# Dilated local attention as banded 121-key matmuls with an unshifted exp, in place of VectorE products over shifted keys

## Chip, core, metric

One NeuronCore of a Trainium2 chip (trn2). The metric is the device time of one execution in microseconds; the kernel before takes 307.15 us (median of 4 runs, 306.28 to 307.87).
A *state* is given with each run: fast or slow. A single core shows a slow state in a few executions here (342.45 against 337.4 to 338.3 us for the changed kernel). Only fast runs are compared.
A ratio below is, as far as it can be recomputed, the mean time of an experiment's fast runs over that of the kernel before in the same rounds on the same chip, without the profiled run, so it is not quite the ratio of the medians that are quoted.

## The reference, cut to what matters

2048 tokens of 448 features; 16 heads of 28. Every query sees 8 keys: itself and the tokens 2, 4, ... 14 before it.

```python
def _A_ref(x, wqkv, wo):                      # attention
    H = 16; Dh = D // H; W, dil = 8, 2
    q, k, v = split(x @ wqkv)
    idx = pos[:, None] - arange(W)[None, :] * dil
    logits = einsum("bhsd,bhswd->bhsw", q, k[idx]) * Dh ** -0.5   # masked where idx < 0
    o = einsum("bhsw,bhswd->bhsd", softmax(logits), v[idx])
    return merge(o) @ wo

def _B_ref(x, w1, w2, w3, w4):                # mixer and MLP
    h = gelu(layernorm(x) @ w1)
    hs = concat(four quarters of h, shifted by +1, -1, +2, -2 tokens) @ w2
    x1 = x + hs
    return x1 + gelu(layernorm(x1) @ w3) @ w4

h  = x + _A_ref(layernorm(x), A_wqkv, A_wo)
h2 = h + _B_ref(layernorm(h), B_w1, B_w2, B_w3, B_w4)
```

## The kernel before

Instructions are not written in the order in which they run. Each helper (`mm`, `act`, `dve`, `pool`, `dma`) puts an operation with an *estimated duration* on a list; a list scheduler then fixes one static order per engine, and semaphores are derived from it. Each engine's program holds its instructions in that order, whatever the real durations are.

Attention of a tile of 512 tokens:

```python
        def phase_A2(t):
            for c in range(4):           # q times 8 shifted copies of k: one 112x4096 product each
                dve("tensor_tensor", 4096, out=ring(slot)..., in0=q_b, in1=k_s, op=ALU.mult)
            for c in range(4):           # sum over the 28 features of a head, with an indicator matrix
                for a8 in range(8):
                    mm(L, zc[:, c, ...], ring(slot)[:, a8 * 512:(a8 + 1) * 512], first, last, 512)
            # row maximum, subtract, exp, sum, reciprocal of 128x64, scale ...
            dma(..., Pd[t * 128:(t + 1) * 128, :], pb[:, sl, :], 128 * 1024)   # probabilities to memory
            # ... and back, each row copied to the 28 partitions of its head (64 loads of 224 KB)

        def phase_A3(t):
            for c in range(4):           # probabilities times 8 shifted copies of v
                dve("tensor_tensor", 4096, out=r4, in0=r4, in1=v_s, op=ALU.mult)
            for c in range(4):           # sum over the 8 keys: identity matmuls
                for w in range(NW):
                    mm(ps[0:KC, b, :], ident[0:KC, 0:KC], r4[:, :, w, :], w == 0, w == NW - 1, 512)
                act(actT[:, a, c, :], ps[0:KC, b, :], ACT.Copy, 512)
            # ... output projection with wo; x is added by one more identity matmul
```

Layer norms use three Newton steps of tiny VectorE instructions for the inverse deviation, and ScalarE for the normalisation. Part B (`B1`: w1 and gelu, `B2`: w2, residual, statistics, `W3`: w3 and gelu, `B3`: w4 and output) begins on the first tiles while attention of the last is still under way.

## Time and profile before

| | before |
|---|---|
| time, median | 307.15 us |
| last attention result written | about 171 us |
| matmuls of part B dense | from 206 us |
| mean granted TensorE clock | 0.961 |

The page of the profiled execution: the busy time, the slices (40 equal slices of the span, each digit the busy share of a slice in tenths, PEclk the granted TensorE clock in tenths) and the chain that ended last.

```profile
span 306.6 us, 3389 instructions
...
PE 260.6 (85%) x1297; PEld 136.4 (44%) x1297; DVE 168.8 (55%) x346; ACT 154.7 (50%) x240; POOL 19.7 (6%) x44
...
PE   0499959959995799996777988949899999989996
...
DVE  3659889983799728985762789001801640200221
...
PEclk9999979979999599998999999986999999999999
...
PE 53%; DVE 27%; ACT 15%; issue 3%; DMA 1%
```

TensorE is busy nearly everywhere. VectorE is busy in the first half and idle in the second. Groups of instructions, shapes kept apart (busy us, mean ns of one, then idle time before them and its releasers):

```profile
L630 DVE TENSOR_TENSOR arena<-arena 112x4096 bf16<-112x4096 bf16 x32 | 72.0, 2287 | 17.6 <-PE ps L630 9.5 <-DMA arena<-attn_p_scratch 7.5 <-ACT arena L630 0.3
...
L630 DVE RECIPROCAL rz<-zs 128x64 f32<-128x64 f32 x4 | 2.2, 553 | 0.1
```

The second line is small here: a reciprocal of 64 columns takes 553 ns. Two windows (length; busy time of PE, PEld, DVE, ACT, POOL with the number of instructions; granted clock; DMA share; GB/s): attention from 25 to 171 us, and the last part.

```profile
25.00:171.00 146.00, 124.10 (x597) 66.76 (x596) 111.12 (x179) 78.46 (x125) 0.21 (x2) 0.94 0.55 127
...
206.00:304.00 98.00, 94.85 (x488) 46.92 (x486) 24.59 (x66) 41.59 (x65) 12.07 (x12) 0.97 0.06 18
```

Attention and the start of part B share the first window, and TensorE is 85% busy in it (124.10 of 146).

### The profile page before, as it was taken

What the parts mean: (1) busy time and instruction counts of PE and PEld (TensorE: products, weight loads), DVE (VectorE), ACT (ScalarE), POOL (GpSimd) and SP (SyncE); (2) the same over time, 40 slices, a digit from 0 to 9 for tenths busy, and PEclk for the clock granted to TensorE, in tenths of its full rate; (3) what the DMA queues carried; (4) which work ended last, traced back from release to release, by engine and by line L of the source; (5) the groups of instructions that cost most, each with busy time, mean ns of one, the idle gap of its engine ahead of it and who ended that gap; (6) DMA issues with size and microseconds to landing.
All of it is one profiled execution on the core that took longest, in us unless ns stands there. A gap on an engine that the chain in (4) does not pass through costs nothing.

```text
span 306.6 us, 3389 instructions
## 1 busy us (share of the span) xinstructions
PE 260.6 (85%) x1297; PEld 136.4 (44%) x1297; DVE 168.8 (55%) x346; ACT 154.7 (50%) x240; POOL 19.7 (6%) x44
## 2 busy tenths in 40 slices
PE   0499959959995799996777988949899999989996
PEld 0254435526542365452444554425445544544552
DVE  3659889983799728985762789001801640200221
ACT  1522346446730567524897568695663167066000
POOL 4000000000000000000000005002205002300000
PEclk9999979979999599998999999986999999999999
DMA  7900018837850299915885000000000100100111
GB/s 224 327 4 0 3 32 202 197 84 175 195 112 0 63 200 207 205 33 145 196 178 191 0 0 2 0 1 0 2 0 30 33 0 0 47 15 0 32 45 45
DMA packets 11824, 24.71 MB, mean 81 GB/s; under 512 B 1376, under 2 KB 9120, under 8 KB 10016
## 3 DMA queue, kind: packets, MB, share of 16 engines
q1 hardware_dynamic: 11808, 24.50, 32.6%
q8 instruction: 10, 0.16, 0.2%
q14 instruction: 6, 0.05, 0.1%
HBM read 22.13 MB, written 2.36 MB: 80 GB/s over the span
## 4 chain that ended last, share of the span: by engine, by line
PE 53%; DVE 27%; ACT 15%; issue 3%; DMA 1%
PE ps L630 53%; DVE arena L630 17%; ACT actT L630 7%; ACT lntm L630 4%; ACT arena L630 3%; DVE st L630 3%; DVE rs_t L630 1%; DVE rs_y L630 1%; DMA xin<-in_A_x_dram 1%; DVE mv L630 1%; DVE ls L630 1%; ACT ls L630 1%; DVE mx L630 1%; ACT L630 0%; DVE rs_x L630 0%
## 5 line engine op out<-in xcount | busy, mean ns | idle before, releaser
L630 PE MATMUL ps<-actT,arena 112*128 112x512 bf16 (+1 forms) x416 | 100.8, 404 | 17.2 <-ACT actT L630 16.6
L630 ACT ACTIVATE arena<-ps 112x512 bf16<-112x512 f32 (+1 forms) x114 | 68.0, 597 | 46.4 <-PE ps L630 46.3
L630 DVE TENSOR_TENSOR arena<-arena 112x4096 bf16<-112x4096 bf16 x32 | 72.0, 2287 | 17.6 <-PE ps L630 9.5
L630 PEld LDWEIGHTS ps<-actT,arena 112*128 112x128 bf16 (+1 forms) x416 | 48.7, 121 | 66.7 <-ACT actT L630 22.2
L630 ACT ACTIVATE actT<-ps 112x1024 bf16<-112x1024 bf16 (+1 forms) x40 | 32.6, 846 | 29.5 <-PE ps L630 29.5
L630 DVE TENSOR_TENSOR ost<-ps,arena 128x448 bf16<-128x448 f32 x16 | 10.0, 625 | 64.6 <-PE ps L630 64.6
L630 PE MATMUL ps<-arena 128*128 128x448 bf16 x224 | 42.9, 353 | 0.0
L630 ACT ACTIVATE lntm<-xin,nbias,rs_y 128x448 bf16<-128x448 bf16 x32 | 22.9, 750 | 17.6 <-DVE nbias L630 17.6
L630 PEld LDWEIGHTS ps<-arena 128*128 128x128 bf16 x224 | 21.9, 98 | 20.7
L630 PE MATMUL ps<-arena,ident 112*112 112x512 bf16 x128 | 28.8, 380 | 0.8 <-DVE arena L630 0.8
L630 PE MATMUL ps<-arena,zc 112*128 112x512 bf16 x128 | 28.3, 380 | 0.0
L630 DVE BATCH_NORM_STATS2 st<-xin 128x6 f32<-128x448 bf16 x32 | 19.3, 604 | 15.6 <-ACT xin L630 11.0
L630 PE MATMUL ps<-ident,lntm 128*112 128x128 bf16 x192 | 15.5, 229 | 13.9 <-ACT lntm L630 13.8
L630 POOL TENSOR_TENSOR arena<-arena,xin 128x448 f32<-128x448 f32 x16 | 16.1, 1035 | 110.8 <-ACT lntm L630 110.8
L630 PE MATMUL ps<-wo_s,actT 112*128 112x448 bf16 x64 | 17.2, 379 | 6.7 <-ACT actT L630 6.4
L630 PE MATMUL ps<-actT,w_s 112*112 112x512 bf16 x64 | 18.6, 441 | 4.6 <-ACT actT L630 4.6
L630 PEld LDWEIGHTS ps<-arena,ident 112*112 112x112 bf16 x128 | 16.5, 130 | 11.9 <-DVE arena L630 1.3
L630 PEld LDWEIGHTS ps<-ident,lntm 128*112 128x112 bf16 x192 | 14.0, 136 | 17.2 <-ACT lntm L630 15.0
L630 DVE TENSOR_TENSOR arena<-ps,arena 128x448 f32<-128x448 f32 x16 | 9.6, 599 | 21.7 <-PE ps L630 21.6
L630 PEld LDWEIGHTS ps<-arena,zc 112*128 112x128 bf16 x128 | 12.4, 98 | 15.0 <-issue 0.2
L630 ACT ACTIVATE ls<-ls 128x512 f32<-128x512 f32 x4 | 2.5, 630 | 28.4 <-DVE ls L630 28.4
L630 PEld LDWEIGHTS ps<-actT,w_s 112*112 112x112 bf16 x64 | 9.0, 150 | 12.2 <-ACT actT L630 6.6
(39 smaller groups left out, 134.4 us busy)
## 6 DMA issues: line engine op xcount, KB each, us to landing
arena<-attn_p_scratch SPq DMA_DIRECT2D x64, 224.0 KB
arena<-in_B_w_dram SPq DMA_DIRECT2D x2, 1568.0 KB, 11.5
xin<-in_A_x_dram SPq DMA_DIRECT2D x4, 448.0 KB, 8.2
out_dram<-ost SPq DMA_DIRECT2D x16, 112.0 KB, 1.7
arena<-in_A_wqkv_dram SPq DMA_DIRECT2D x1, 1176.0 KB, 7.4
w_s<-in_B_w_dram SPq DMA_DIRECT2D x2, 392.0 KB, 8.8
attn_p_scratch<-pb SPq DMA_DIRECT2D x4, 128.0 KB, 1.8
wo_s<-in_A_wo_dram SPq DMA_DIRECT2D x1, 392.0 KB, 10.3
```

The source lines that it names most:

```text
L630: inst = getattr(eng, op.meth)(**op.kw)
```

## The change

The intent: take attention off VectorE and out of memory. Tokens are split into even and odd ones, so that the 8 keys of a query are 8 neighbours of the same parity. A block of 114 queries then needs 121 keys. One *unit* is 3 blocks for 4 heads; 2 parities x 3 groups x 4 channels of heads make 24 units. Per unit TensorE computes full 121x114 scores, exp is taken without a row maximum, a 0/1 mask keeps the band, and two sets of matmuls give the outputs and, replicated over 32 partitions, the sums. If an intermediate leaves the floating-point range, a flag sends every engine into the old program, which is kept behind a branch. The core of the diff:

```diff
+    ring = {"st": [(0, 1, 2, 3), 0], "oz": [(4, 5), 0], "gen": [(6, 7), 0]}     # the 8 PSUM banks
+    def phase_att(par, g):
+        for c in range(4):
+            for blk in range(3):                       # scores: 12 matmuls, 28 rows each
+                for j in range(4):
+                    mm(ps[0:KB, j, blk * QB:(blk + 1) * QB], kT[32 * j:32 * j + 28, ...],
+                       qT[32 * j:32 * j + 28, ...], True, True, 40)
+            act(pt[0:KB, sl, :, :], ps[0:KB, 0:4, 0:GQ], ACT.Exp, 4 * GQ, scale=SCALE)
+            dve("tensor_tensor", 4 * GQ, 2.0, out=pt..., in0=pt..., in1=m_, op=ALU.mult)
+            bo, bz = bank("oz"), bank("oz")
+            # ... outputs into bo: 12 matmuls (121 rows, 32 columns of weights, 114 moving)
+            # ... sums into bz: 12 matmuls of the same shape, with ones as weights
+            dve("reciprocal", GQ, psum=True, out=rzb[:, u % 2, :], in_=ps[:, bz, 0:GQ])    # GQ = 342
+            dve("scalar_tensor_tensor", GQ, psum=True, out=oT..., in0=rzb[:, u % 2, :],
+                scalar=UP, in1=ps[:, bo, 0:GQ], op0=ALU.mult, op1=ALU.mult)
 ...
+    phase_att(0, 0)
+    phase_QK(1)
+    phase_V(1, 0)
+    phase_A1(2)
+    phase_att(1, 0)
+    phase_QK(2)
 ...                                    # all six attention phases, then
+    for t in range(NST):
+        phase_B1(t)
+    # flag from the exponent bits of the statistics
+    phase_B2(0)
+    phase_B2(1)
+    phase_W3(0)
 ...
+                        emit_fast(e, eng)
+                        eng.wait_ge(flag_op.sem, flag_op.val)
+                        with eng.register("redo_" + e) as reg:
+                            eng.reg_load(reg, flag[0:1, 0:1])
+                            with eng.If_ne(reg, 0):
+                                # ... the old program
```

Besides, the inverse deviation becomes a power on GpSimd, normalisation moves from ScalarE to VectorE, and the weights of part B are loaded at the start. The scheduler is told 523 ns for the reciprocal.

## The prediction

> **What bounds it now.** The busy table gives PE 260.6 us (85%), VectorE 168.8, ScalarE 154.7 of a 306.6 us span; the chain of waits is 53% matmuls, 27% VectorE, 15% ScalarE. The last attention result is written at about 171 us (timeline; part B starts overlapping it at 147). In it VectorE is nearly saturated (windows 20-60 and 80-100 us: 19 of 20 us busy), mainly the 32 products of 112x4096 (2287 ns each, 72.0 us in all). From 206 us on, matmuls are dense (94.9 of 98 us).
>
> **Removed.** The 32 large VectorE products (72 us), max/subtract/sum/scale (about 12 us), the 128+128 reducing and summing 512-column matmuls, 16 residual matmuls, the scratch round trip through memory (14 MB read back), the Newton chains (about 25 us of tiny VectorE instructions, now a power on GpSimd). A dense chain of 166 matmuls took 33.03 us, 199 ns each; so the 256 reduction matmuls are about 51 us of PE time. The normalisations leave ScalarE (45 us) for VectorE in a faster mode (estimate 0.27 us bf16, 0.35 us f32: 20 us).
>
> **Added: 24 units (2 parities x 3 groups x 4 channels).** Costs, estimated from trace durations:
> - PE: 36 small matmuls, each with its weights. Sixteen transpose pairs of like size took 1.05 us, 66 ns each; so 2.4 us without concurrency, perhaps 1.5 us with it: 36-57 us in all. The Trainium skill (TensorEngine Tiling, Key Properties) says changing tiling mode drains the engine; no run shows it yet.
> - ScalarE: exp of 121x1368; evictions of 512 and 1024 columns (597, 1016 ns) give 170 ns + 0.82 ns a column: 1.3 us, 31 us in all.
> - VectorE: mask 0.87 us (2287 ns scaled); product with the inverse 0.5 us; and the reciprocal. The trace has 128x64 at 553 ns where an instruction on four columns takes 162: over 6 ns a column. The Trainium skill (VectorE: DVE Perf Modes, the fixed hardware budget) says reciprocal is an iterative divide, repeat count 8; the trace agrees in kind. For 342 columns: about 2.3 us, not the 0.5 us that the new scheduler is told; 55 us in all. VectorE per unit: 3.7 us, 90 us in all.
>
> **Where it lies.** One pair of output/sum banks serves all units, so each waits for the reciprocal and product of the one before: mask, 24 matmuls, reciprocal, product form a loop of 4.5-5 us; VectorE fills its gaps with statistics and residual adds (about 27 us). Attention becomes VectorE-bound: about 25 us of start plus 24 x 4.8, ending near 140 us instead of 171. Then part B: about 125 us of matmuls, as before, with eight banks: 125-132 us. Flag, register load and skipped branch: an estimated 2-4 us.
>
> **Prediction: 266 us, range 238 to 290.** Faster by over 2%: 0.91; within 2%: 0.06; slower: 0.03.
>
> **What would show it.** Reciprocal near 2.3 us and VectorE 170-185 us busy in total; in the attention stretch VectorE over 85% busy and the loop reciprocal, product, matmul in the chain; PE total about 215-235 us; no DMA between 30 us and the outputs; part B about 130 us, PE-bound.
>
> **What would make it wrong.** A reciprocal that scales better than its 64-column time says: then attention is PE-bound, 235-245 us. Small matmuls that don't overlap, with mode drains and a throttled clock: attention at 6 us a unit, 290. The static order stalling the in-order PE. Slow GpSimd powers. A dear branch at the end.

## More of the kernel before

```python
    def schedule(self, dma_bw=170.0, slack=2000.0):
        # ... for each engine, among operations whose predecessors are placed:
        for op in ready[e]:
            st = rdy_t[op.idx] if rdy_t[op.idx] > fr else fr
            # take the earlier start, but prefer the lower program index
            # as long as it starts within `slack` ns of the earliest
            ...
```

So with `slack=2000.0` an engine idles up to 2 us (in the scheduler's estimate) rather than take an operation that comes later in the program.

What TensorE waited for between 30 and 145 us (total us, times, longest):

```profile
PE ps L630 <- ACT actT L630: 15.4, 5, 5.7
PE ps L630 <- ACT lntm L630: 0.4, 1, 0.4
```

## The result, and the profile after

338.19 us median (fast runs 337.38 to 338.30, one slow run of 342.45) against 307.15: ratio 1.0994, 95% interval 1.0959 to 1.1029. The change makes the kernel 10% slower; the forecast was 13% faster. The result is correct, and the fast path ran: the other one never shows in the trace.

```profile
span 335.7 us, 4428 instructions
...
PE 236.4 (70%) x1897; PEld 119.5 (36%) x1897; DVE 179.8 (54%) x284; ACT 131.5 (39%) x176; POOL 45.2 (13%) x81
...
PE   0596287279249439615535978749999989989994
...
DVE  3673770771583788599699670891360271200221
...
PEclk9998589579659955957557799958999999999999
...
PE 56%; DVE 28%; ACT 11%; DMA 2%; issue 1%; SPq 0%
```

TensorE has 24 us less to do than before, and the span is 29 us longer. Its digits swing between 1 and 9 in slices 4 to 20, and the clock swings with them. The groups of a unit, shapes apart:

```profile
L991 DVE RECIPROCAL rzb<-ps 128x342 f32<-128x342 f32 x24 | 55.0, 2292 | 15.1 <-PE ps L991 15.0
...
L991 ACT ACTIVATE pt<-ps 121x1368 bf16<-121x1368 f32 x24 | 31.5, 1311 | 72.0 <-PE ps L991 72.0
...
L991 DVE TENSOR_TENSOR pt<-pt,msk 121x1368 bf16<-121x1368 bf16 x24 | 20.8, 866 | 24.0 <-ACT pt L991 24.0
...
L991 DVE SCALAR_TENSOR_TENSOR oT<-rzb,ps 128x342 bf16<-128x342 f32 x24 | 12.3, 511 | 0.8
```

These sizes are as forecast (2.3, 1.3, 0.87, 0.5 us). Now one unit in order of time (start, length, engine, instruction, how often; in brackets the idle time before it and who ended it):

```profile
63.71 0.48 PE L991 MATMUL ps<-pt,arena 121*32 121x114 bf16 x12 [3.52 <-DVE pt L991]
...
63.97 0.50 PE L991 MATMUL ps<-pt,ones 121*32 121x114 bf16 x12
...
64.40 0.56 PE L991 MATMUL ps<-arena 28*121 28x114 bf16 x12
...
64.81 2.30 DVE L991 RECIPROCAL rzb<-ps 128x342 f32<-128x342 f32 x1 [1.16 <-PE ps L991]
65.22 1.31 ACT L991 ACTIVATE pt<-ps 121x1368 bf16<-121x1368 f32 x1 [3.47 <-PE ps L991]
67.14 0.51 DVE L991 SCALAR_TENSOR_TENSOR oT<-rzb,ps 128x342 bf16<-128x342 f32 x1
67.57 0.87 DVE L991 TENSOR_TENSOR pt<-pt,msk 121x1368 bf16<-121x1368 bf16 x1
68.48 0.23 PEld L991 LDWEIGHTS ps<-pt,arena 121*32 121x32 bf16 x12 [3.70 <-DVE pt L991]
```

Output and sum matmuls, the next unit's scores, then the reciprocal (2.30), the product (0.51), the next mask (0.87), and only then the next output matmuls: 63.71 to 68.49, a period of 4.78 us, in which TensorE works about 1.2 us and stands still for 3.5. That is the loop that was forecast, in its forecast size. What was not forecast is what lies between two groups of four units. The chain of waits, in order of time, at one such place:

```profile
71.92 0.51 DVE oT L991
72.43 0.79 DVE pt L991
73.26 8.21 PE ps L991 x57
81.49 2.47 ACT arena L991 x3
83.96 1.21 ACT pt L991
85.19 0.88 DVE pt L991
```

The block of 8.21 us begins with the 24 output and sum matmuls of the group's fourth unit; behind them the projections of the next tile and its transposes run in one piece; then ScalarE evicts the last of them, and the loop starts again. The next three lines are windows: a group's loop, the block after it, and the whole attention half.

```profile
58.00:73.00 15.00, 6.31 (x114) 3.45 (x114) 11.43 (x10) 5.02 (x5) 0.00 (x0) 0.54 0.01 1
73.00:85.00 12.00, 10.29 (x90) 5.03 (x90) 3.01 (x3) 8.18 (x12) 0.00 (x0) 1.00 0.01 2
...
31.00:183.00 152.00, 84.80 (x1096) 43.23 (x1096) 105.17 (x119) 55.96 (x66) 7.56 (x14) 0.70 0.00 1
183.00:225.00 42.00, 31.42 (x183) 18.35 (x183) 27.49 (x68) 19.31 (x27) 6.85 (x10) 0.87 0.00 1
225.00:331.00 106.00, 102.68 (x528) 49.84 (x528) 29.98 (x51) 40.13 (x63) 18.37 (x19) 0.98 0.05 17
```

VectorE works while TensorE waits, and TensorE works while VectorE waits (11.43 of 15, then 3.01 of 12). TensorE's waits between 30 and 183 us, against the 15.8 us of before:

```profile
PE ps L991 <- DVE pt L991: 62.1, 24, 4.0
PE ps L991 <- DVE oT L991: 3.6, 3, 2.7
```

Where the time went, from the starts of the 24 products that write the outputs: the first is at 35.18 us and the last ends at 183.1. The 18 distances within groups average 4.75 us; the 5 between groups are 12.91, 12.91, 14.34, 12.04 and 9.80 us, together 38 us more than five periods of 4.78. Part B then takes from 183.1 to 331.3 us (the end of the last VectorE instruction), 148 us, of which the first 42 are thin.

### The profile page after: what moved, and what is told of

It is laid out like the page before. It is cut to its first block, busy times and chain, and to the rows that moved or that the text cites. A ratio compares the mean times of both kernels' runs of the same rounds, so it can differ in the third digit from the quotient of the medians.

```text
span 335.7 us, 4428 instructions
## 1 busy us (share of the span) xinstructions
PE 236.4 (70%) x1897; PEld 119.5 (36%) x1897; DVE 179.8 (54%) x284; ACT 131.5 (39%) x176; POOL 45.2 (13%) x81
## 4 chain that ended last, share of the span: by engine, by line
PE 56%; DVE 28%; ACT 11%; DMA 2%; issue 1%; SPq 0%
PE ps L991 56%; DVE rzb L991 14%; DVE pt L991 6%; ACT actT L991 4%; ACT arena L991 4%; DVE oT L991 3%; DVE st L991 3%; ACT pt L991 2%; DMA arena<-in_A_wqkv_dram 2%; DVE arena L991 1%; DVE mv L991 1%; DVE xin L991 1%; SPq L991 0%; DVE lntm L991 0%; DVE ost L991 0%
## 5 line engine op out<-in xcount | busy, mean ns | idle before, releaser
L991 ACT ACTIVATE arena<-ps 128x512 bf16<-128x512 f32 (+3 forms) x130 | 79.5, 616 | 47.5 <-PE ps L991 47.5
L991 PE MATMUL ps<-actT,w_s 112*128 112x512 bf16 (+1 forms) x288 | 67.0, 389 | 6.6 <-ACT actT L991 6.5
L991 PE MATMUL ps<-arena 28*121 28x114 bf16 (+2 forms) x488 | 65.7, 349 | 2.8 <-ACT arena L991 2.7
L991 DVE RECIPROCAL rzb<-ps 128x342 f32<-128x342 f32 x24 | 55.0, 2292 | 15.1 <-PE ps L991 15.0
L991 ACT ACTIVATE pt<-ps 121x1368 bf16<-121x1368 f32 x24 | 31.5, 1311 | 72.0 <-PE ps L991 72.0
L991 PE MATMUL ps<-w_s,arena 128*128 128x448 bf16 (+1 forms) x288 | 55.3, 352 | 0.0
L991 PEld LDWEIGHTS ps<-actT,w_s 112*128 112x128 bf16 (+1 forms) x288 | 29.3, 106 | 41.7 <-ACT actT L991 12.0
L991 PEld LDWEIGHTS ps<-arena 28*121 28x121 bf16 (+2 forms) x488 | 30.1, 159 | 34.4 <-ACT arena L991 12.3
L991 PEld LDWEIGHTS ps<-w_s,arena 128*128 128x128 bf16 (+1 forms) x288 | 28.1, 98 | 26.4
L991 DVE TENSOR_TENSOR pt<-pt,msk 121x1368 bf16<-121x1368 bf16 x24 | 20.8, 866 | 24.0 <-ACT pt L991 24.0
```

The costliest lines, as they stand in the source:

```text
L991: inst = getattr(eng, op.meth)(**op.kw)
```

## The experiments

Theory A: the reciprocal sets the period of a loop through one pair of PSUM banks, and the static order puts the projections (and the start of part B) in series with it. Theory B, the rival that the clock of 0.54 in the loop suggests: the attention half is slow because TensorE is throttled and its small tiled matmuls are dear. Rival C: the branch and the second program cost the time. Every kernel here was timed in three rounds and gives a correct result unless said otherwise.

### A copy in place of the reciprocal

```diff
-            dve("reciprocal", GQ, psum=True, out=rzb[:, u % 2, :], in_=ps[:, bz, 0:GQ])
+            dve("tensor_copy", GQ, psum=True, out=rzb[:, u % 2, :], in_=ps[:, bz, 0:GQ])
```

> Edit: the reciprocal of 128x342 becomes a copy of the same columns (wrong result on purpose), with the same planned duration, so the order of instructions stays as it is on every engine. Theory A (the 2.29 us reciprocal sets the period of a loop through one pair of PSUM banks, and the projection matmuls stand in blocks between the loops, in series with them): the copy takes about 0.5 us, the period falls from 4.78 to about 3.0 us, 24 x 1.8 = 43 us go, total about 295 us; the blocks between groups (37 us in excess of the period) stay. Theory B (the throttled TensorE clock and the small tiled matmuls slow the attention half): the period is mostly PE time, so 5 to 15 us go, total 322 to 333.

Measured: 312.99 us, ratio 1.0177 (1.0139 to 1.0215), wrong result. 25 us less than the changed kernel, not 43. The reciprocal counts, so B in its pure form falls, but the period stops at 3.78 us. One unit of this run in order of time:

```profile
59.79 0.48 PE L991 MATMUL ps<-pt,arena 121*32 121x114 bf16 x12 [2.92 <-DVE pt L991]
...
60.05 0.51 PE L991 MATMUL ps<-pt,ones 121*32 121x114 bf16 x12
...
60.49 0.56 PE L991 MATMUL ps<-arena 28*121 28x114 bf16 x12
...
60.89 0.51 DVE L991 COPY rzb<-ps 128x342 f32<-128x342 f32 x1 [1.15 <-PE ps L991]
61.30 1.31 ACT L991 ACTIVATE pt<-ps 121x1368 bf16<-121x1368 f32 x1 [2.46 <-PE ps L991]
61.44 0.51 DVE L991 SCALAR_TENSOR_TENSOR oT<-rzb,ps 128x342 bf16<-128x342 f32 x1
62.64 0.87 DVE L991 TENSOR_TENSOR pt<-pt,msk 121x1368 bf16<-121x1368 bf16 x1 [0.69 <-ACT pt L991]
```

Now the mask waits for exp (0.69 us idle before it), where it had waited for VectorE itself. A second loop was hidden under the first: scores stand *behind* the output matmuls on TensorE, then exp, then mask, then the next output matmuls: 3.78 us. Of the 1.78 us that the copy saves, 1.0 shows within a group: the 18 distances there lose 17.5 us together. The five distances between groups lose 4.3 us, nearly all in the last two. An earlier first product (33.31 instead of 35.18 us) and 0.9 us in part B make most of the rest.

### The true cost of the reciprocal, told to the scheduler

```diff
-            dve("reciprocal", GQ, psum=True, ...)
+            S.add("dve", "reciprocal", 2290.0, ...)
```

> Edit: only the duration that the static scheduler is told for the reciprocal, 523 to 2290 ns; the instructions are the same. In the new order TensorE still has the projection matmuls after each group of four units; the scores are computed one unit further ahead and masks move before reciprocals. Theory A, in its form that the block order comes from the 2 us slack of the scheduler and not from the wrong cost: total 320 to 338 us. If the wrong cost alone caused the serial blocks: about 300. Theory B: no change, 334 to 342.

Measured: 325.43 us, ratio 1.0593 (1.0559 to 1.0627), 12 us less. The order changes a little (scores one unit ahead for the second unit of each group, whose period falls to 3.99 us), but the blocks stay: distances between groups 12.0, 12.0, 13.9, 9.1 and 6.9 us. So correcting the cost alone gains 12 us, and the smaller slack in the next run another 21. A smaller slack with the wrong cost was not run, so the share of each is known in this sequence only.

### True cost, and a slack of 200 ns

```diff
-    order = S.schedule()
+    order = S.schedule(slack=200.0)
```

> Edit: true cost of the reciprocal and a scheduler slack of 200 ns in place of 2000 ns; the instructions are the same, but projection matmuls now stand between the scores and the output matmuls of each unit. Theory A: most of the 37 us of excess between groups is hidden in the loop's waits, total 295 to 305 us, PE idle in the attention stretch falls, and the loop period of about 4.8 us becomes the floor (24 x 4.8 = 115 us). Theory B: the matmul time itself is the cost, so hiding it behind waits gains under 10 us: 328 to 340.

Measured: 304.37 us, ratio 0.9914 (0.9887 to 0.9941), 34 us less than the changed kernel with not one instruction changed. Projections now stand between the matmuls of the units: the last product of attention ends at 139.8 us instead of 183.1, the distances between groups fall to 5.8 to 8.6 us, and most distances within groups to 3.6 us. The last product of the changed kernel, the last of this run, and this run's window over attention:

```profile
182.60 0.51 DVE L991 SCALAR_TENSOR_TENSOR oT<-rzb,ps 128x342 bf16<-128x342 f32 x1
...
139.31 0.51 DVE L991 SCALAR_TENSOR_TENSOR oT<-rzb,ps 128x342 bf16<-128x342 f32 x1
...
31.00:140.00 109.00, 82.53 (x1094) 39.09 (x1092) 94.09 (x87) 54.45 (x67) 0.17 (x2) 0.84 0.01 1
```

VectorE is busy 94.09 of 109 us here (86%), where the changed kernel had 105.17 of 152 (69%); TensorE does nearly the same work (82.53 against 84.80 us) in 43 us less. This is the run that decides for the order. The whole gain is in attention; part B now takes 158 us.

### TensorE kept warm

```diff
+            bd = bank("gen")
+            for _ in range(8):
+                S.add("pe", "matmul", 1.0, out=ps[:, bd, :], lhsT=ident[0:KC, :],
+                      rhs=wqkv_s[:, 0, 0:512], start=True, stop=True)
             act(pt[0:KB, sl, :, :], ps[0:KB, 0:4, 0:GQ], ACT.Exp, 4 * GQ, scale=SCALE)
```

> Edit: eight useless 512-column matmuls per unit (192 in all) into a free bank, in the place where TensorE waits for the mask; the order of everything else stays. They keep the clock up. Theory A: the granted clock in the attention stretch rises from 0.55-0.9 to about 0.95, but the period falls only by what the 24 small output matmuls lose to the clock, 0.3 to 0.5 us of 4.78: total 323 to 336. Theory B: if the low clock is the cause, most of the loss goes: 295 to 310.

Measured: 336.9 us, ratio 1.0977 (1.0946 to 1.1008), 1 us less. The window that the changed kernel spent at a clock of 0.70:

```profile
31.00:183.00 152.00, 121.13 (x1284) 55.20 (x1276) 104.88 (x119) 56.29 (x66) 7.56 (x14) 0.91 0.00 1
```

The clock is 0.91, TensorE is busy 36 us longer in the window, and the last product starts at 181.98 us instead of 182.60. Counted from the first product (34.22 and 35.18 us), the stretch even takes 147.8 us against 147.4. The clock rises when the waits are filled, and the time hardly changes: the low clock follows from the waits and causes next to nothing. Theory B falls; the small matmuls by themselves are sized below.

### Without the branch and the old program

```diff
-                        emit_fast(e, eng)
-                        eng.wait_ge(flag_op.sem, flag_op.val)
-                        with eng.register("redo_" + e) as reg: ...
+                        emit_fast(e, eng)
```

> Edit: the flag test, the branch and the whole old program are taken out; the fast path is left as it is, instruction for instruction. Theory A: the exit costs only what the profile's end shows, 4.4 us from the last VectorE instruction to the end against 2.2 us before: 2 to 3 us less, 335 to 336.5. Rival C (the second program in the instruction stream and the branch cost much): below 330.

Measured: 335.54 us, ratio 1.0914 (1.0868 to 1.0960; one of four runs slow). About 2.5 us less (mean of the fast runs 335.4 against 337.9 us, in other rounds); after the last VectorE instruction the profile has 2.1 us instead of 4.4. Rival C falls.

### The copy with scores ahead

```diff
-            dve("reciprocal", GQ, psum=True, ...)
+            S.add("dve", "tensor_copy", 2290.0, ...)     # the order of the true-cost run
```

> Edit: copy in place of reciprocal (wrong result on purpose) in the order that computes the scores one unit ahead (the order of the run with the true cost, 325.4 us). The first copy run gained 25 us and not 43, its period stopping at 3.77 us; theory A2 says a second loop took over there (scores after output matmuls, exp, mask, output matmuls). With the scores ahead that loop is out of the way, so the full 24 x 1.78 = 43 us should go: about 283, range 278 to 292. If A2 is wrong and something else holds the period near 3.7: 300 to 312.

Measured: 308.13 us, ratio 1.0043 (1.0000 to 1.0086), wrong result. A miss: 17 us below the true-cost run, not 43. The distances in the first group tell why: 4.66, 2.22, 4.96 us, where the true-cost run had 4.78, 3.99, 4.72. Only the second unit of a group has its scores ahead in this order, and there the period fell by the whole 1.77 us. The first still waits for scores, exp and mask; before the last stand ten projection matmuls. So the second loop is confirmed where the order takes it away, and my reading of the order was careless.

### The copy in the interleaved order

```diff
+            S.add("dve", "tensor_copy", 2290.0, ...)
+    order = S.schedule(slack=200.0)
```

> Edit: copy in place of reciprocal (wrong result on purpose) in the interleaved order of the slack run (304.4 us). There the units of a group follow each other at 3.6 us, nearly all VectorE work (0.87 + 2.29 + 0.51). If the reciprocal still bounds that order, VectorE falls by 43 us and the period to 2.0 to 2.8: 270 to 288. If projections and exp now bound it: less than 10 us gained, 295 to 303.

Measured: 285.92 us, ratio 0.9293 (0.9262 to 0.9324), wrong result; 18 us below the slack run, between the two expectations. Most distances within the first groups fall from 3.6 only to 3.2 or 3.3 us. Probably other work fills them, since the order is still made for a reciprocal of 2.29 us; no run tests that. What the reciprocal is worth depends on the order around it: 25, 17 and 18 us in the three orders tried, never the 43 us that its instructions got shorter by.

### Part B alone

Attention is left as it is, with the wrong cost and the 2 us slack. Only the program order after it changes.

```diff
-    for t in range(NST):
-        phase_B1(t)                   # statistics, transposes and w1 matmuls, tile by tile
-    phase_B2(0)
-    phase_B2(1)
-    phase_W3(0)
+    phase_B1(0); phase_B1(1); phase_B1(2)      # statistics, normalisation, transposes only
+    phase_B1b(0); phase_B1(3); phase_B1b(1); phase_B1b(2)      # B1b: w1 matmuls and gelu
+    phase_B2(0)
+    phase_B1b(3)
+    phase_W3(0)                                # normalisation and transposes
+    phase_B2(1)
+    phase_W3b(0)                               # w3 matmuls and gelu
 ...
```

> Edit: the changed kernel with its attention half untouched (same order of TensorE there, wrong cost and 2 us slack kept), and only part B's program order changed: transposes of the four tiles together, projections after them, B2 of the first tile before the last projection, the normalisation for W3 before the next tile's B2. No instruction changes. Theory A's part-B half (about 20 us of part B are serial VectorE and GpSimd chains): 10 to 18 us less than the changed kernel, 320 to 328. If part B is bound by matmuls or by the low clock after attention: 334 to 340.

Measured: 326.43 us; two of four runs were slow, the fast ones are 323.6 and 324.35 us, 13.9 us less than the fast runs of the changed kernel. The ratio, 1.0621 (1.0539 to 1.0703), still counts the run of 328.52 us; the two fast runs over the mean of the kernel before (307.36 us) give 1.054. The last product of attention starts at 182.81 us as before (182.60), so all of it is part B: 133.9 us instead of 148.2 in the profile. In the 42 us after attention TensorE is busy for 37.79 us, where the changed kernel had 31.42:

```profile
183.00:225.00 42.00, 37.79 (x214) 22.02 (x215) 31.02 (x70) 23.98 (x36) 12.84 (x15) 0.92 0.00 1
```

Some 14 of the 148 us were waits that an order takes away.

### Everything by order

True costs for the main operations, 60 ns for a hand-over from one engine to another, slack 200 ns, and statistics and transposes of part B's first three tiles put into the program among the attention phases; no instruction changes.

```diff
     phase_WO(0)
+    phase_B1(0)
     phase_att(1, 1)
 ...
     phase_WO(2)
+    phase_B1(2)
     phase_att(1, 2)
 ...          # then part B as in the run above
```

> Edit: no instruction changes, only order: true durations for the scheduler, slack 200 ns, statistics and transposes of part B's first three tiles put in the program between attention groups, the inverse deviation that is needed first computed first, B2 and W3 interleaved. Theory A with its part-B half (about 20 us of part B are serial chains of VectorE and GpSimd with TensorE idle, not matmul work): attention ends near 140 us and part B takes about 130: 268 to 283. If part B is bound by matmuls: no better than the slack run, 300 to 305.

Measured: 286.75 us, ratio 0.9317 (0.9283 to 0.9352), 51 us below the changed kernel. It missed its range of 268 to 283 by 4 us: attention ended at 157.3 us and not near 140, because it now also carries work of part B, and from there to the last VectorE instruction (280.6 us) it took 123 us.

### The mask on TensorE

As the last, with slack 100 ns, and the mask as a term of the scores:

```diff
+            for j in range(4):
+                mm(ps[0:KB, j, 0:GQ], ident[0:KB, 0:KB], msk[0:KB, 0 if g == 0 else 1, :], True, False, GQ)
             # scores: start=False; msk holds 0 and -30000
-            dve("tensor_tensor", 4 * GQ, 2.0, out=pt..., in0=pt..., in1=m_, op=ALU.mult)
```

> Edit: as the order run, and the mask is added to the scores by four 342-column matmuls per unit (14 us of TensorE in all) in place of the VectorE product after exp (20.8 us); slack 100 ns. If VectorE bounds the attention stretch once the order is right: 255 to 270, at least 5 us below the order run. If TensorE bounds it: no better than the order run, or up to 8 us worse.

Measured: 279.64 us, ratio 0.9084 (0.9045 to 0.9123): 7 us below the order run and 9% faster than the kernel before, though short of the 255 to 270 expected. Mask and slack were changed together, so the 7 us are not split between them. This version beats both kernels. Its page, and TensorE's longest waits from 30 to 152 us (16 us in all), where the changed kernel had 66 us:

```profile
span 277.9 us, 4617 instructions
...
PE 241.0 (87%) x1993; PEld 126.7 (46%) x1993; DVE 161.4 (58%) x260; ACT 129.1 (46%) x176; POOL 46.2 (17%) x81
```

```profile
PE ps L1013 <- ACT pt L1013: 8.2, 5, 1.7
PE ps L1013 <- DVE rzb L1013: 6.8, 10, 2.0
...
```

Five of the kernels here run the same instructions and differ only in their order: 338.2 (the changed kernel), 325.4 (true cost), 324.0 (part B alone, mean of two fast runs), 304.4 (slack) and 286.8 us (everything by order). In these runs the order is worth up to 51 us, the reciprocal at most 25.

## Why the prediction was wrong

Right, with their sizes:
- "For 342 columns: about 2.3 us": 2292 ns. Mask 866, product 511, exp 1311 ns, VectorE 179.8 us busy against the "170-185" of the prediction. The Trainium skill (VectorE: DVE Perf Modes, "First, the fixed hardware budget") says that reciprocal is an iterative divide; from 64 to 342 columns the trace shows (2292 - 553) / 278 = 6.3 ns a column.
- "mask, 24 matmuls, reciprocal, product form a loop of 4.5-5 us": 4.78 us.
- "Flag, register load and skipped branch: an estimated 2-4 us": about 2.5 us, by taking them out.
- Small matmuls were forecast at 36 to 57 us; from the first output matmul to the reciprocal, with the next scores issued in between, a unit takes about 1.1 us (63.71 to 64.81), so about 26 us in all. The 24 weight-and-matmul pairs of outputs and sums started within 0.46 us at the low clock (31.75 to 32.21) and within 0.28 us at the full one (46.07 to 46.35). The error was on the harmless side. The drain at a change of tiling mode, which the Trainium skill states (TensorEngine Tiling, Key Properties), shows at most as the 0.10 to 0.18 us for which the weight loads stand idle between sums and scores.

Wrong, and this turns faster into slower: **"Attention becomes VectorE-bound: about 25 us of start plus 24 x 4.8, ending near 140 us".** The sum has no term for the projections, transposes and output projections that TensorE must do for attention besides the units (264 matmuls at the 199 ns of the dense chain and 64 transposes at 66 ns, an estimate of 57 us; 212 and 32 of them, an estimate of 44 us, start in the trace between the first output matmul at 31.75 us and the end of attention at 183.1): I took for granted that they fit into the loop's 3.5 us of TensorE idle time per unit. The engines execute a static order; the scheduler had planned with a 0.52 us reciprocal and a 2 us preference for program order, and so put those matmuls in blocks between the groups. Loop and projections ran one after the other: 38 us, and the start took 5 us longer (first product at 35.2 us, where 25 plus one period made 29.8; why was not tested). Attention ended at 183 us, and it was not VectorE-bound: VectorE was busy 69% of it, where the prediction wanted over 85%. The slack run, with the true cost told, puts the matmuls into the gaps without a change of instruction; VectorE is then 86% busy and attention ends at 139.8 us. That this is the forecast's 140 is in part luck: the run starts later (first product at 35.5 us) and most of its periods are shorter (3.6 us). The prediction had this under what would make it wrong ("The static order stalling the in-order PE") but gave it no time. It was readable: the slack is in the code, the durations told to the scheduler were compared with the trace for one instruction only, and a wait shorter than the slack in its own estimate is never filled.

Mis-sized: **"Then part B: about 125 us of matmuls, as before, with eight banks: 125-132 us".** It took 148. In the kernel before, the first layer norms of part B run beside the last tile of attention (part B's first matmuls at 147 us, attention's last result at 171). The new program starts them all behind attention, where each tile is a serial chain of transposes, eviction, projections and gelu, and the first W3 waits for 8 add-and-statistics steps. With another order of the same instructions, 14 us went (part B alone); with its first stages moved among the attention phases, part B took 123 us, just under the forecast size. What the other 6 of the 20 us were in the changed kernel was not isolated.

The two terms and the start make 5 + 38 + 20 = 63 of the 70 us by which the profiled span exceeds 266. The rest is the exit of 4.4 us after the last VectorE instruction and an error of addition: the prediction's own terms, 140, 125 to 132 and 2 to 4 us, make 267 to 276 us, and not 266.

The relation between the two loops and the order is shown where the order was changed; the exact worth of the reciprocal alone stays open, since it was 17 to 25 us in three orders and none of them was made for the shorter instruction.

## What to carry to other kernels

When the order of instructions is fixed beforehand, a bound by engine ("VectorE-bound, 24 x 4.8 us" here) holds only if the order lets the other engines work in that engine's shadow: look at what stands behind each long wait in the in-order stream, and add what cannot run there to the sum. A low TensorE clock beside long waits can be their effect and not their cause, as here; filling the waits with useless matmuls tests it in one run. And give a scheduler measured durations and a slack smaller than the gaps it should fill.

## What the Trainium skill lacked or had wrong

- VectorE: DVE Perf Modes names the iterative divide of reciprocal but gives no time: 553 ns for 128x64 and 2292 ns for 128x342 f32, 6.3 ns a column (the first reads SBUF, the second PSUM), where a copy of the same 342 columns takes 511 ns.
- TensorE: Matmul & The Clock Gate, Part 1, says that starts of matmuls never come closer than about 25 ns however small they are. Twelve column-tiled matmuls with their weights started within 0.13 us here (46.07 to 46.20): three fours, some 2 to 6 ns between the starts in a four and 42 to 51 ns between fours. Its Part 3, about tiles running concurrently at some 4 ns between starts, fits better; the floor of Part 1 does not hold for these tiled matmuls.
- TensorEngine Tiling (Array Packing), Key Properties, states the drain at a change of tiling mode without a size: between the sums (121x32 weights) and the scores (28x121) the weight loads stood idle 0.10 to 0.18 us here, which bounds this one change.
